# One core: routing one-hots of five groups on GpSimd, copies of the transposed inverse and of the scores on ScalarE

## The chip, the core and the metric

The program runs on one core of one Trainium2 chip. Four engines compute in it: TensorE (PE in the rows; its weight loads are PEld), VectorE (DVE), ScalarE (ACT) and GpSimd (POOL). SyncE (SP) issues most of the transfers. Each engine works through its own list of instructions strictly in order and waits on semaphores for the others. The metric is the device time of one execution in microseconds (us), the median of several runs. Less is better.

## What is computed

Three stages follow one another; the second needs all of the first only through the routing, and the third needs the second.

```python
# 1. delta-rule attention: 4 batches, 8 heads, 768 steps, head width 48
for t in range(S):
    kt, vt, bt = k_n[:, :, t], v[:, :, t], beta[:, :, t, None]
    y[:, :, t] = einsum('bhd,bhde->bhe', q[:, :, t], state)
    v_old = einsum('bhde,bhd->bhe', state, kt)
    state = state + bt[..., None] * einsum('bhd,bhe->bhde', kt, vt - v_old)
# 2. mixture of 8 experts, one expert for a token, tokens with x @ w_skip <= 0 pass through
out[do_compute] = xc + gate * (relu(xc @ w1[e]) @ w2[e])     # e = argmax(xc @ w_gate)
# 3. a wide layer over all 3072 tokens
h = relu(x @ w_in);  return (h * h) @ w_out
```

## The kernel before

**Attention.** The 768 steps are cut into 12 chunks of 64, and two chunks make a group, so there are six groups, 0 to 5. The recurrence inside a chunk is turned into a triangular system. For each group the program needs the inverse of 32 x 32 triangular blocks, all of them at once across the 128 partitions. `inv(g,jj)` builds it row by row on VectorE: 31 steps, each of them a multiplication into `it` (L213) and a subtraction from `T` (L214), and every one waits for the one before it. `T` is first set to the identity by two GpSimd memsets (L195), and its buffer is the one in which `Dg` stood, so the memsets wait for the transposition `At` (L188) that reads `Dg`. After the last step `back` transposes `T` to `X` (L226) and scales it (L227); `back3` transposes it again to `Tn` (L234) and then copies `Tn` in eight pieces into `TX` (L238): four quadrants `qd`, two chunks `j`. `mg` makes the off-diagonal blocks in two rounds of small matmuls: the first (L249) needs `X`, ScalarE copies its result to `M` (L254), and the second (L251) needs `M` and `TX`. `e1` (L260) and `e2` (L272) then make the matrices of each chunk, `sstep` (L288) and `ystep` (L301) carry the state and the output, and `xnat` (L307) brings the output of one batch of the group into token order.

**Two groups ahead** the same loop prepares keys and queries: `norm` (L114 to L124, mostly on GpSimd, from `raw`, a single buffer that a SyncE transfer fills, L88), `scale` (L130), `kp` (L138), `trk`, `trq`, `gp` (L172, with the mask L177 on GpSimd behind the copy L176).

**Routing.** `xnat` ends in `scores` (L435, a sum over the heads on VectorE), a copy of the nine scores of each token into `xn` (L309) and a copy of the token itself (L310); `xn` goes to memory by L311. When all four batches of a group are there, `group` finds the expert of each token: `oh` (L447), then `rk` by matmul (L450 to L454), the rank of each token (L457), and then two rounds, h = 0 and 1, of four one-hot tiles `O` (L466, 128 x 128 in f16, `is_equal` of an iota with the rank). Each `O` is the weight of two small matmuls into `pi` (L468). `O` has one buffer, so the second round waits for the matmuls of the first. `pi` is added to `slots` (L469). The routing of group g stands among the work of group g+1; that of group 5 stands at the end of the attention, and the first gather of the experts waits for it.

**What sets the order.** `PLANS` gives the order in which the pieces of a group are written, `merge` interleaves them with the 31 steps of the next inverse by `WEIGHT`, and then the framework's scheduler sorts the instructions of every engine by a timeline of its own. So whoever moves one instruction to another engine also moves others. `nc.any` leaves the engine to the framework; it divided the 48 copies at L238 into 24 on ScalarE and 24 on VectorE.

**Experts and wide layer.** From about 400 us on, matmuls on TensorE fill the time (L582 to L584, three products for each, for the split of f32 into two parts).

Of the kernel before, what the change touches and what calls it, by code (L numbers as in the profile page):

```python
# [6 lines left out]
B,H,S,D=4,8,768,48  # L7
# [7 lines left out]
WEIGHT={'e': 1.67, 'f': 0.255, 'T': 0.057, 'Q': 0.295, 'G': 6.868, 'S': 1.411, 'Y': 2.496, 'X': 2.685}  # L15
NL=5
NPOOL=1
ENG='gggv v aaav'.split()
KX0='a'; KT0=1; TQ0=0; CA=3; CS=13
EARLY=2  # L20
C=64; NCH=S//C; NG=NCH//2; PR=H//2; BP=B*PR
# [39 lines left out]
def attention(tc, q,k,v,beta, xd, c, scores, group_done):  # L61
    nc=tc.nc
    ident,mU,mb,i48=c['ident'],c['mU'],c['mb'],c['i48']
    with ExitStack() as ctx:
# [7 lines left out]
        TX=P1.tile([128,2,BP,2,64],F32,name="tx")  # L72
# [11 lines left out]
        def e_(x): return {'v':nc.vector,'g':nc.gpsimd,'a':nc.any}[x]  # L84
# [54 lines left out]
        def kxload(g,j,bh):  # L139
            ch=2*g+j  # L140
            for hp in range(2):
                r=slice(64*hp,64*hp+64)
                e_(ENG[0][(2*j+bh)%len(ENG[0])] if g else KX0).tensor_copy(KX[ch%2][r,HB[bh],64*(1-hp):64*(1-hp)+D],ST[ch]['KP',bh][r,:,0:D])
        def trk(g,b):
# [75 lines left out]
        def back(g):  # L220
# [5 lines left out]
            nc.vector.transpose(X.rearrange("p c i -> p i c"),T)  # L226
            e_(ENG[1] if g else 'v').tensor_tensor(T,T,bm.unsqueeze(1).to_broadcast([128,32,32]),op=ALU.mult)  # L227
            st['X']=X
        def back3(g,qd):
            T=G[g]['T']; hp,blk=qd//2,qd%2; r=slice(32*qd,32*qd+32)  # L230
            tn=G[g].setdefault('Tn',None)
            if tn is None:
                tn=P1.tile([128,2*BP,32],F32,tag="sq",name=f"Tn{g}")
                G[g]['last']=nc.vector.transpose(tn.rearrange("p c m -> p m c"),T.rearrange("p i m -> p m i"))  # L234
                G[g]['Tn']=tn
            for j in range(2):
                ST[2*g+j]['TX']=TX[:,j]
                e_(ENG[2][qd] if g else 'a').tensor_copy(TX[r,j,:,hp,32*blk:32*blk+32],tn[r,j*BP:(j+1)*BP])  # L238
        def mg(g,bh):
            st=G[g]; H8=HB[bh]; pp=pE if g==0 and bh else pM  # L240
            for stage in (1,2):
# [61 lines left out]
        def xnat(g,b):  # L303
            xT=G[g]['xT']; last=g==NG-1
            tp=pS.tile([128,PR,128],F32,tag="mm",name=f"tx{g}_{b}")
            for p in range(PR):
                nc.tensor.matmul(tp[:,p,0:105],xT[:,b*PR+p],c['RW'][:,p],start=True,stop=True)  # L307
            xn=P2.tile([128,DX],F32,tag="E2",name=f"xn{g}_{b}")
            nc.vector.tensor_copy(xn[:,DM:],scores(g,b,tp[:,:,96:105]))  # L309
            nc.scalar.copy(xn[:,0:DM].rearrange("p (a d) -> p a d",d=2*D),tp[:,:,0:2*D])  # L310
            c['lastx']=nc.sync.dma_start(xd[0:B*S].rearrange("(b g t) f -> g b t f",b=B,t=128)[g,b],xn)  # L311
            if b==B-1: group_done(g,pS,P2)
# [42 lines left out]
        for qd in range(4): back3(0,qd)  # L355
# [62 lines left out]
class Routing:  # L418
# [14 lines left out]
    def scores(s,g,b,ps):  # L433
        if g not in s.lg: s.lg[g]=s.P.tile([128,B,9],F32,tag="lg",name=f"lg{g}")
        s.nc.vector.tensor_reduce(s.lg[g][:,b],ps.rearrange("p a e -> p e a"),axis=AX.X,op=ALU.add)  # L435
        return s.lg[g][:,b]
    def group(s,g,P,pm,P2):
        nc,rc,V=s.nc,s.rc,s.nc.vector; lg=s.lg[g]; H2=CAP//128; E9=E+1
        def t(n,sh,dt=F32): return P.tile(sh,dt,tag=n,name=f"{n}{g}")
# [6 lines left out]
        r=t('r',[128,B]); V.tensor_reduce(r,val,axis=AX.X,op=ALU.max)  # L446
# [16 lines left out]
        pi=pi[:,0:H2*E].rearrange("p (a b) -> p a b",b=E)  # L463
        for h in range(H2):
            O=P.tile([128,B,128],F16,tag="O",name=f"OH{g}_{h}")
            for b in range(B): V.tensor_scalar(O[:,b],rc['io'][:,128*h:128*h+128],s.rank[:,g,b:b+1],None,op0=ALU.is_equal)  # L466
            for b in range(B):
                for w in range(2): nc.tensor.matmul(pi[:,h],O[:,b],rh[:,b,w],start=b==0 and w==0,stop=b==B-1 and w==1)  # L468
        s.last=V.tensor_tensor(s.slots if g<NG-1 else s.idx,s.slots,pi,op=ALU.add)  # L469
# [453 lines left out]
```

## Time and profile before

| what | value |
|---|---|
| three runs | 989.68, 991.57 (median), 996.97 us |
| the profiled execution | 987.27 us, of which 985.5 us lie between the first and the last instruction (the span) |
| busy: TensorE, VectorE, ScalarE, GpSimd | 880.8, 634.2, 454.1, 278.3 us |
| mean granted TensorE clock | 0.938 of full speed |
| six routings: one-hots at L466 | 48 on VectorE, 240/248/751 ns least/median/most |

The rows further down come from the page and the trace of the profiled execution. Times are in us from the start of the span. "Busy" is the time in which an engine executed something; "x" is a count. In a row of waits, the engine and the line that waited stand left of the arrow, and what ended the wait stands right of it. POOLq, DVEq and SPq are the sequencers that issue for these engines.

### The profile page before, as it was taken

What the parts mean: (1) busy time and instruction counts of PE and PEld (TensorE: products, weight loads), DVE (VectorE), ACT (ScalarE), POOL (GpSimd) and SP (SyncE); (2) the same over time, 40 slices, a digit from 0 to 9 for tenths busy, and PEclk for the clock granted to TensorE, in tenths of its full rate; (3) what the DMA queues carried; (4) which work ended last, traced back from release to release, by engine and by line L of the source; (5) the groups of instructions that cost most, each with busy time, mean ns of one, the idle gap of its engine ahead of it and who ended that gap; (6) DMA issues with size and microseconds to landing.
All of it is one profiled execution on the core that took longest, in us unless ns stands there. A gap on an engine that the chain in (4) does not pass through costs nothing.

```text
span 985.5 us, 20218 instructions
## 1 busy us (share of the span) xinstructions
PE 880.8 (89%) x7820; PEld 814.9 (83%) x7820; DVE 634.2 (64%) x1546; ACT 454.1 (46%) x913; POOL 278.3 (28%) x395
## 2 busy tenths in 40 slices
PE   3369799988989888599999999999999999999994
PEld 3369689878878787589999899899999999998994
DVE  6798999988797922597887999633533433433332
ACT  4455466646654332366566577523332332333221
POOL 7676754353221100576313120220200300200001
PEclk9776988989999959599999999999999999999997
DMA  6773766857664625776857676310100200100000
GB/s 102 95 96 61 141 112 135 144 122 144 125 125 95 138 50 134 260 252 203 277 198 245 208 233 201 101 54 1 53 14 1 65 1 1 41 1 8 25 0 35
DMA packets 182134, 105.83 MB, mean 107 GB/s; under 512 B 154086, under 2 KB 166406, under 8 KB 182034
## 3 DMA queue, kind: packets, MB, share of 16 engines
q1 hardware_dynamic: 150418, 76.73, 32.3%
q0 software_dynamic: 5504, 16.75, 5.3%
q10 hardware_dynamic: 26112, 11.02, 5.3%
q8 instruction: 64, 1.05, 0.5%
q14 instruction: 36, 0.29, 0.1%
HBM read 60.85 MB, written 19.06 MB: 81 GB/s over the span
## 4 chain that ended last, share of the span: by engine, by line
PE 37%; issue 14%; DVE 6%; DMA 4%; ACT 2%; POOL 1%; SPq 0%; POOLq 0%; ACTq 0%; DVEq 0%
PE mh L582 4%; PE mh L584 4%; PE mh L583 4%; PE o L583 4%; PE o L584 4%; PE o L582 4%; PE h L582 2%; PE h L584 2%; PE h L583 2%; PE y L584 2%; PE y L582 2%; PE y L583 2%; DMA raw<-in_moe_w_dram 2%; PE e L260 1%; DVE wl L563 1%
## 5 line engine op out<-in xcount | busy, mean ns | idle before, releaser
L736 DVE TENSOR_TENSOR r<-r 128x512 f32<-128x512 f32 x80 | 55.4, 692 | 169.6 <-ACT gh L735 166.0
L733 ACT ACTIVATE r<-mh 128x512 f32<-128x512 f32 x96 | 57.3, 597 | 212.3 <-PE mh L584 204.9
L583 PE MATMUL o<-wl,gh 128*128 128x384 f32 x384 | 128.8, 338 | 0.0
L582 PE MATMUL o<-wh,gh 128*128 128x384 f32 x384 | 128.4, 337 | 0.0
L582 PE MATMUL mh<-x2h,wh 128*128 128x512 f32 x288 | 115.6, 401 | 0.5 <-ACT r L733 0.5
L583 PE MATMUL mh<-x2l,wh 128*128 128x512 f32 x288 | 113.1, 393 | 0.0
L584 PE MATMUL mh<-x2h,wl 128*128 128x512 f32 x288 | 112.9, 394 | 0.0
L413 POOL DMA_INDIRECT out_dram<-os,rows x24 | 24.4, 1017 | 297.6 <-DVE os L762 236.8
L584 PE MATMUL o<-wh,gl 128*128 128x384 f32 x384 | 89.7, 337 | 0.0
L582 PEld LDWEIGHTS o<-wh,gh 128*128 128x128 f32 x384 | 72.0, 188 | 3.6
L583 PEld LDWEIGHTS o<-wl,gh 128*128 128x128 f32 x384 | 72.0, 188 | 3.5
L584 PEld LDWEIGHTS o<-wh,gl 128*128 128x128 f32 x384 | 69.8, 188 | 3.3 <-DVE gl L737 0.2
L737 DVE TENSOR_TENSOR gl<-r,gh 128x512 fp32r<-128x512 f32 x96 | 66.3, 690 | 5.5
L213 DVE TENSOR_TENSOR it<-At,T 128x31 f32<-128x31 f32 (+15 forms) x155 | 64.3, 415 | 8.3 <-POOL T L195 5.4
L563 DVE TENSOR_TENSOR wl<-raw,wh 128x512 fp32r<-128x512 f32 x96 | 63.1, 700 | 5.9 <-ACT wh L562 4.9
L172 PE MATMUL gp<-KQ,ktx 128*128 128x128 f32 x384 | 57.8, 306 | 8.5 <-ACT ktx L155 6.0
L214 DVE TENSOR_TENSOR T<-T,it 128x31 f32<-128x31 f32 (+15 forms) x155 | 62.9, 406 | 3.3
L260 PE MATMUL e<-KP,tx 128*128 128x112 f32 x384 | 62.0, 315 | 1.5 <-ACT E L262 1.0
L735 ACT ACTIVATE gh<-r 128x512 fp32r<-128x512 f32 x96 | 60.9, 635 | 2.3
L584 PEld LDWEIGHTS mh<-x2h,wl 128*128 128x128 f32 x288 | 53.9, 188 | 9.6
L582 PEld LDWEIGHTS mh<-x2h,wh 128*128 128x128 f32 x288 | 54.2, 188 | 9.1 <-ACT r L733 1.3
L172 PEld LDWEIGHTS gp<-KQ,ktx 128*128 128x128 f32 x384 | 52.4, 216 | 10.6 <-ACT ktx L155 6.6
(253 smaller groups left out, 2081.7 us busy)
## 6 DMA issues: line engine op xcount, KB each, us to landing
raw<-in_moe_w_dram SPq DMA_DIRECT2D x30, 768.0 KB
L<-E ACTq DMA_DIRECT2D x96, 112.0 KB
raw<-in_moe_w_out_dram SPq DMA_DIRECT2D x16, 384.0 KB
L<-E SPq DMA_DIRECT2D x48, 112.0 KB
xd<-xn SPq DMA_DIRECT2D x24, 196.5 KB
raw<-in_k_dram SPq DMA_DIRECT2D x24, 192.0 KB
qn<-in_q_dram SPq DMA_DIRECT2D x12, 384.0 KB
KP<-kn SPq DMA_DIRECT2D x48, 96.0 KB
```

Of the source, the lines that this page charges most:

```text
L172: nc.tensor.matmul(ps[:,p],w,KQ[:,j,p],start=True,stop=True)
L213: e.tensor_tensor(tv,At[:,jj,jj+1:32].unsqueeze(2).to_broadcast([128,n,m]),T[:,jj,0:m].unsqueeze(1).to_broadcast([128,n,m]),op=ALU.mult)
L214: return e.tensor_tensor(T[:,jj+1:32,0:m],T[:,jj+1:32,0:m],tv,op=ALU.subtract)
L260: nc.tensor.matmul(ps[:,p,0:112],st['TX'][:,b*PR+p].rearrange("p h t -> p (h t)"),st['KP',b//2][:,b%2*PR+p],start=True,stop=True)
L563: eng.tensor_tensor(lo[:,sl],r[:,sl],f32v(hi)[:,sl],op=ALU.subtract)
L582: nc.tensor.matmul(out,ah,bh,start=first,stop=False)
L583: nc.tensor.matmul(out,ah,bl,start=False,stop=False)
L584: return nc.tensor.matmul(out,al,bh,start=False,stop=last)
L733: nc.scalar.activation(r,pp,AF.Relu)
L735: nc.scalar.activation(gh,r,AF.Square)
L736: z=nc.vector.tensor_tensor(r,r,r,op=ALU.mult) if n else nc.scalar.activation(r,r,AF.Square)
L737: (nc.gpsimd if n==0 and GLP=='g' else nc.vector).tensor_tensor(gl,r,f32v(gh),op=ALU.subtract)
```

## The change

It does four things. At L466 the one-hots of groups 0 to 4 are made by GpSimd; those of group 5 stay on VectorE. At L238 the copies of quadrants 0, 1 and 2 go to ScalarE by name and those of quadrant 3 to VectorE, for groups 1 to 5 (group 0 is left to the framework as before). At L309 the copy of the scores into `xn` goes from VectorE to ScalarE. A table `ENG` loses the entry that the new lines replace.

```diff
-ENG='gggv v aaav'.split()
+ENG='gggv v'.split()
...
-                e_(ENG[2][qd] if g else 'a').tensor_copy(TX[r,j,:,hp,32*blk:32*blk+32],tn[r,j*BP:(j+1)*BP])
+                o,i=TX[r,j,:,hp,32*blk:32*blk+32],tn[r,j*BP:(j+1)*BP]
+                if g==0: nc.any.tensor_copy(o,i)
+                elif qd<3: nc.scalar.copy(o,i)
+                else: nc.vector.tensor_copy(o,i)
...
-            nc.vector.tensor_copy(xn[:,DM:],scores(g,b,tp[:,:,96:105]))
+            nc.scalar.copy(xn[:,DM:],scores(g,b,tp[:,:,96:105]))
...
-            for b in range(B): V.tensor_scalar(O[:,b],rc['io'][:,128*h:128*h+128],s.rank[:,g,b:b+1],None,op0=ALU.is_equal)
+            for b in range(B): (V if g==NG-1 else nc.gpsimd).tensor_scalar(O[:,b],rc['io'][:,128*h:128*h+128],s.rank[:,g,b:b+1],None,op0=ALU.is_equal)
```

The lines behind L238 stand three lower in the changed kernel (L466 is L469 there). VectorE's list loses 10 of its 24 copies at L238, so that 14 are left there and 34 stand on ScalarE. The lists of all engines differ from the routing of group 0 on. Three places matter below.

GpSimd, where the inverse of group 2 has been used and that of group 3 begins (`KP_1` are masks for the keys of group 4, `T_2631` is the `T` of group 3, `raw_2617` and `sq` belong to the norm of group 5). Before:

```order
L130 TENSOR_TENSOR kn<-raw_1787,ss_2327 128x16x48
L177 TENSOR_TENSOR KP_1_2176<-KP_1_2176,mU 128x4x64
L177 TENSOR_TENSOR KP_1_2179<-KP_1_2179,mU 128x4x64
L195 MEMSET T_2631 128x1024
L195 MEMSET T_2631 128x32
L114 TENSOR_TENSOR sq_0_2743<-raw_2617 128x768
L115 TENSOR_TENSOR sq_0_2743<-sq_0_2743 128x16x24
```

And the same engine and place in the changed kernel:

```order
L114 TENSOR_TENSOR sq_0_2743<-raw_2617 128x768
L115 TENSOR_TENSOR sq_0_2743<-sq_0_2743 128x16x24
L115 TENSOR_TENSOR sq_0_2743<-sq_0_2743 128x16x12
L115 TENSOR_TENSOR sq_0_2743<-sq_0_2743 128x16x6
L115 TENSOR_TENSOR sq_0_2743<-sq_0_2743 128x16x3
L116 TENSOR_TENSOR sq_0_2743<-sq_0_2743 128x16
L117 TENSOR_TENSOR ss_2742<-sq_0_2743 128x16
L114 TENSOR_TENSOR sq_8_2758<-raw_2617 128x768
L177 TENSOR_TENSOR KP_1_2176<-KP_1_2176,mU 128x4x64
L177 TENSOR_TENSOR KP_1_2179<-KP_1_2179,mU 128x4x64
L195 MEMSET T_2631 128x1024
```

The first half of the norm of group 5 and the first operation of its second half now stand ahead of the two masks and of the memsets of `T`; the second memset follows three rows later, behind an L115 and an L121. On SyncE the four transfers into `raw_2617` moved ahead of the loads of `qn` and `z`, behind which they stood.

ScalarE at the same boundary, behind the transposition `Tn` of group 2 (`M_2_0` are the copies between the two rounds of small matmuls). Before:

```order
L292 COPY z_178<-s_1_2135 48x8x48 x2
L254 ACTIVATE M_2_0_2471<-m_2_0_0_2469 32x512
L254 ACTIVATE M_2_0_2471<-m_2_0_1_2470 32x512
L238 COPY tx<-Tn_2459 32x16x32 x4
L176 COPY KP_1_2176<-gp_3_2443 128x4x64
L302 COPY xT_1914<-y_1_2156 128x8x64
```

And now:

```order
L160 COPY KQ_3_2273<-tq_3_2317 128x4x2x64
L162 COPY QT_3_2323<-tq_3_2317 128x4x2x64
L240 COPY tx<-Tn_2459 32x16x32 x6
L257 ACTIVATE M_2_0_2471<-m_2_0_0_2469 32x512
L257 ACTIVATE M_2_0_2471<-m_2_0_1_2470 32x512
L305 COPY xT_1914<-y_1_2156 128x8x64
L312 COPY xn_0_2187<-lg_2188 128x9
```

The copies of `Tn` are six and stand ahead of `M`; before, they were four and stood behind it.

TensorE at the routing of group 2, among the work of group 3 (`pi` with `OH_0`, the first round; `s_1` is the state). Before:

```order
L288 MATMUL s_1_3270<-z_178,L_164 48x48 x7
L468 LDWEIGHTS OH_0_3226
L468 MATMUL pi_3225<-rh_3222,OH_0_3226 128x8
L468 LDWEIGHTS OH_0_3226
L468 MATMUL pi_3225<-rh_3222,OH_0_3226 128x8
L468 LDWEIGHTS OH_0_3226
L468 MATMUL pi_3225<-rh_3222,OH_0_3226 128x8
```

And now:

```order
L291 MATMUL s_1_3270<-z_178,L_166 48x48 x3
L252 MATMUL m_3_1_1_3373<-X_3185,A_1942 32x32
L252 MATMUL m_3_1_1_3373<-X_3185,A_1941 32x32
L252 MATMUL m_3_1_1_3373<-X_3185,A_1942 32x32
L263 MATMUL e_6_0_3447<-KP_0_1935,tx 128x112 x2
L471 LDWEIGHTS OH_0_3226
L471 MATMUL pi_3225<-rh_3222,OH_0_3226 128x8
L471 LDWEIGHTS OH_0_3226
L471 MATMUL pi_3225<-rh_3222,OH_0_3226 128x8
L263 MATMUL e_6_0_3447<-KP_0_1935,tx 128x112 x2
L263 MATMUL e_7_0_3467<-KP_0_1938,tx 128x112 x4
```

The pairs of `pi` matmuls, one pair for each one-hot tile, stood together and are now spread between other matmuls.

## Rows read from the trace of the kernel before

**Rows 1.** Busy by stretch: PE, PEld, DVE, ACT, POOL; then clock, DMA share, GB/s
```profile
80.00:133.00 53.00, 46.67 (x596) 43.37 (x595) 47.49 (x106) 27.66 (x58) 30.61 (x50) 0.83 0.65 117
294.00:345.00 51.00, 44.41 (x814) 40.88 (x812) 42.44 (x127) 22.10 (x45) 6.77 (x10) 1.00 0.51 113
```
**Rows 2.** VectorE busy by stretch, line 213 alone, then line 214 alone
```profile
80.00:133.00 53.00, 14.65 (x31) 0.83 0.65 117
294.00:345.00 51.00, 10.72 (x31) 1.00 0.51 113
...
80.00:133.00 53.00, 15.87 (x31) 0.83 0.65 117
294.00:345.00 51.00, 10.95 (x31) 1.00 0.51 113
```
**Rows 3.** Line 234, ends of the inverses: ns least/median/most, first and last start
```profile
L234 DVE STREAM_TRANSPOSE Tn<-U x1: 2055/2055/2055, 76.3 to 76.3; 128x1024 f32<-128x1024 f32 x1
L234 DVE STREAM_TRANSPOSE Tn<-T x1: 2080/2080/2080, 130.0 to 130.0; 128x1024 f32<-128x1024 f32 x1
...
L234 DVE STREAM_TRANSPOSE Tn<-T x2: 2072/2082/2093, 291.0 to 341.7; 128x1024 f32<-128x1024 f32 x2
```
**Rows 4.** VectorE busy from 80 to 345: line 466, line 238, line 309
```profile
80.00:345.00 265.00, 6.42 (x32) 0.93 0.63 125
...
80.00:345.00 265.00, 8.86 (x20) 0.93 0.63 125
...
80.00:345.00 265.00, 4.81 (x18) 0.93 0.63 125
```
**Rows 5.** Instructions by line: ns least/median/most, first and last start, forms
```profile
L516 POOL TENSOR_SCALAR ol<-io,lo x24: 590/712/1653, 429.4 to 458.6; 128x128 f16<-128x128 f16 x24
...
L238 ACT COPY tx<-Tn x24: 608/614/619, 78.4 to 345.6; 32x512 f32<-32x512 f32 x24
...
L118 ACT ACTIVATE ss<-ss x10: 215/217/229, 40.8 to 210.1; 128x16 f32<-128x16 f32 x10
```
**Rows 6.** TensorE's waits from 130 to 405: us in total, times, longest
```profile
PE pi L468 <- DVE OH L466: 3.3, 3, 2.0
```
**Rows 7.** Order of time: start, us, engine, line, operation; the first inverse steps of two groups
```profile
140.52 1.47 POOL L114 TENSOR_TENSOR sq<-raw 128x768 f32<-128x768 f32 x1
140.61 1.42 DVE L213 TENSOR_TENSOR it<-At,T 128x31 f32<-128x31 f32 x1 [1.20 <-POOL T L195]
...
193.88 0.19 DVE L213 TENSOR_TENSOR it<-At,T 128x31 f32<-128x31 f32 x1 [1.20 <-POOL T L195]
...
203.80 1.00 DVE L213 TENSOR_TENSOR it<-At,T 128x220 f32<-128x220 f32 x1
```
**Rows 8.** Order of time, 184 to 202: ScalarE, TensorE, GpSimd and SyncE at the boundary
```profile
183.97 2.05 PE L172 MATMUL gp<-KQ,ktx 128*128 128x128 f32 x16
184.34 1.20 ACT L254 ACTIVATE M<-m 32x512 f32<-32x512 f32 x2
185.25 1.48 POOL L130 TENSOR_TENSOR kn<-raw,ss 128x768 f32<-128x768 f32 x1 [0.50 <-PE gp L172]
186.37 2.40 ACT L238 COPY tx<-Tn 32x512 f32<-32x512 f32 x4 [0.83 <-DVE Tn L234]
188.10 1.85 PE L251 MATMUL m<-tx,M 32*32 32x32 f32 x56
189.25 1.86 POOL L177 TENSOR_TENSOR KP<-KP,mU 128x256 f32<-128x256 f32 x2 [2.52 <-ACT KP L176]
190.80 4.78 SPq L88 DMA_DIRECT2D raw<-in_k_dram  x4
192.68 1.16 POOL L195 MEMSET T<- 128x1024 f32 x2 [1.57 <-DVE xn L309]
196.60 1.47 POOL L114 TENSOR_TENSOR sq<-raw 128x768 f32<-128x768 f32 x1 [2.76 <-DMA raw<-in_k_dram]
201.68 1.72 POOL L114 TENSOR_TENSOR sq<-raw 128x768 f32<-128x768 f32 x1
```

## The prediction

> **What bounds the kernel now.** The change touches the attention, the first 400 us, so I read the busy time by stretch first, with one inverse in each stretch. In the first stretch shown TensorE is busy for 46.67 of 53 us and VectorE for 47.49, in the last one for 44.41 and 42.44 of 51; ScalarE has 22 to 28 us, GpSimd 30.61 in the first and 6.77 in the last [rows 1]. So two engines are nearly full, and neither is full: each works through its list in order and waits now and then for the other. Behind 400 us TensorE works on the experts and the wide layer. None of the moved work lies there, so what the attention gains or loses moves the end by the same amount.
>
> The second look is at the inverse, the longest chain on VectorE. Its 31 steps are the same work in every group, and yet the two lines of a step are busy for 14.65 + 15.87 = 30.5 us in the first stretch and for 10.72 + 10.95 = 21.7 us in the last [rows 2]. GpSimd is what differs: 30.61 us of work against 6.77 [rows 1]. The order of time shows how: the first step of one inverse, 128 x 31, takes 0.19 us in one group and 1.42 us in another, where it starts 0.09 us behind a GpSimd operation of 1.47 us and ends with it [rows 7]. That gives a price: (30.5 - 21.7) / (30.61 - 6.77) = 0.37 us of VectorE for one us of GpSimd.
>
> The third look is at what such a loss is worth. From one `Tn` to the next the program takes 130.0 - 76.3 = 53.7 us in the first stretch and 341.7 - 291.0 = 50.7 us in the last [rows 3]. An inverse that is 8.8 us lighter came with a period that is 3.0 us shorter, so 0.34 of what VectorE saves arrives. The stretches differ in other work too, so the true share may be anything from 0 to 1; I take 0.34, because both ends come from the same five periods.
>
> **The change, part by part.** (1) VectorE is relieved. Between 80 and 345 us lie the one-hots of groups 0 to 3, 32 of them, with 6.42 us; 20 copies at L238 with 8.86 us, of which 10 go, 4.4 us; and 18 copies of scores with 4.81 us, which all go [rows 4]. Together 15.6 us. The one-hots of group 4 come behind the last inverse, where VectorE has time, so I count them at nothing on VectorE; if there were no such time, 8 x 0.20 = 1.6 us more would be saved.
>
> (2) GpSimd gets the one-hots. The trace of before has no `is_equal` at L466 there, but it has the same shape and type at L516: 0.59 us at least, 0.71 in the middle, 1.65 at most [rows 5]. In the same stretch that is 32 x 0.71 = 22.7 us more of GpSimd. By the price of 0.37, VectorE gives back 8.4 us. The lower bound is 0 (all one-hots fall beside work that they do not disturb), the upper one a full hold each time, 32 x 0.59 = 18.9 us. I take 8.4, the price that this kernel's own inverses paid. VectorE then keeps 15.6 - 8.4 = 7.2 us, and 0.34 of it arrives: **-2.5 us**, with bounds of -15.6 and +3.3.
>
> What the row shows of the hold in full, a step of 0.19 us that takes 1.42, is what the Trainium skill states as a rule: in "SBUF — State Buffer", section "SBUF: two separate sides", the port pair that VectorE and GpSimd share is a lock held for the whole instruction, and a VectorE operation with two SBUF inputs loses against a GpSimd operation that reads SBUF and started first. By that rule alone every one-hot would hold up an inverse step in full, and this term would be +1.1 us; the trace agrees for the one step and shows 0.37 on average.
>
> (3) TensorE waits for the one-hots in another way. Four tiles took VectorE 4 x 0.20 = 0.8 us and take GpSimd 4 x 0.71 = 2.8 us, so each of the two rounds of a group ends 2.0 us later: 4 us in a group, 20 us in five. Behind a late tile stands TensorE's whole list: the `pi` matmuls wait in order, and with them the state, `e1`, `e2` and the keys. The cover is the work between the pairs, and the new order spreads the pairs for that. In the second round of group 2's routing, 32 small matmuls (1.85/56 = 0.033 us each) and 8 large ones (2.05/16 = 0.13 us each) stand between the last pair of the first round and the last three pairs [rows 8]: 2.1 us against 2.8. So 0.7 us of wait is left in a group, 3.5 in five. Before, this wait was 3.3 us [rows 6]. The difference is **+0.2 us**, with bounds of -3.3 (all covered) and +17 (nothing covered).
>
> (4) The identity for the inverse of group 3 comes later. GpSimd now does the norm of group 5 ahead of the memsets of `T`. The norm needs `raw`; its transfers can go when L130 has read the old content, at 185.25 + 1.48 = 186.7, no longer at 190.80 behind the loads of `qn` and `z`. From issue to the norm's first operation passed 196.60 - 190.80 = 5.8 us, so it starts at 192.5. Its first half takes 201.68 - 196.60 = 5.1 us; then follow 1.72 (second half, first operation), 1.86 (two masks) and 1.16 (memsets): `T` is ready at about 202.3 [rows 8]. The first step stood at 193.88, so it comes 8.4 us later. Some of this returns, for the ten steps up to 203.80 ran under that very norm, in 9.9 us; with 21.7/30.5 of that, 7.0 us, they save 2.9 [rows 2, 7]. The inverse ends 5.5 us later, and with the share of 0.34 that is **+1.9 us**; bounds 0 and +8.4. What is late next is `X` of group 3 and with it the small matmuls of that group.
>
> (5) ScalarE gets 10 x 0.614 = 6.1 us of copies and 24 small ones. For these the nearest row is a 128 x 16 activation with 0.217 us, 5.2 us in all [rows 5]. ScalarE idles half of each stretch, and most of the 11.3 us lies there. One place does not hide it: behind `Tn` of group 2 six copies of 0.60 us now precede `M`, so `M` ends at 186.37 + 3.6 + 1.2 = 191.2, where the second round of small matmuls started at 188.10 [rows 8]. That is 3.1 us later with TensorE's list behind it; again at 0.34, **+1.0 us**, bounds 0 and +3.1. The scores' copy of the last group adds 0.2 us at the end of the attention, which I leave out.
>
> **The sum.** -2.5 + 0.2 + 1.9 + 1.0 = +0.6 us on the profiled execution's 987.27, that is 987.9. That execution lies 4.3 us under the median of the three runs and 2.4 under the lowest; I add half of the 4.3 and forecast **990 us**. About 1%, 10 us, is what a measurement here can tell from no change.
>
> **The rivals.** *VectorE sets the pace (0.20).* Then its 15.6 us arrive in full, the one-hots disturb little, and only the late identity is paid: -15.6 + 1.9 = -13.7, about 976 us. For it: 47.49 of 53 us busy. Against it: the period moved by only 3.0 us where the inverse moved by 8.8 [rows 2, 3].
>
> *Every one-hot holds a step (0.12).* VectorE gives back 18.9 us instead of 8.4, the term is +1.1 instead of -2.5, and the time 994 us. For it stands the step of 1.42 us, against it the average price of 0.37. This is the rule of the page named above.
>
> *The late identity counts in full (0.08).* If the inverse of group 3 sets the pace of its period, +8.4 stands for +1.9: about 997 us. Against it: TensorE has 44 to 47 us of work of its own in a stretch [rows 1].
>
> *TensorE waits for GpSimd's one-hots (0.13).* If nothing covers the 4 us in each of five groups, 20 - 3.3 = 17 us are added: 1007 us, slower. It decides once more than 2.6 us in a group are uncovered, which tiles of 1.2 us would do; at L516 they reach 1.65 [rows 5]. Against it: the pairs stand apart now.
>
> *Forecast (0.47).* The parts cancel as in the sum, 982 to 998 us.
>
> **Chances and range.** Faster by over 1%: the first rival, and a little of the forecast's lower edge: 0.22. Slower by over 1%: the last rival, with the edges of the late identity: 0.17. Within 1%: 0.61. The range goes from 975, near the first rival's time, to 1002, short of the last one's; about 0.2 is left out.
>
> **What would show it.** The one-hots on GpSimd between 0.6 and 0.9 us; a larger mean favours the last rival. The wait of `pi` for `OH` near 3.5 us in all. The first inverse step of group 3 some 8 us behind the end of its `At`, and `M` of group 2 behind six copies. VectorE's two inverse lines heavier by 1 to 3 us in a group. The distance from one `Tn` to the next shorter by half a microsecond to one, and longer from group 2 to group 3. I would be wrong if the distances shrank by 3 us each, or if TensorE's idle time grew at L468.

## The result and the profile of the changed kernel

The changed kernel takes **1001.0 us** (median of 4 runs, 994.3 to 1005.7) where the kernel before, on the same chip, took 990.6. The ratio is 1.0112, with a 95% interval of 1.0069 to 1.0155: slower by about 1.1%. The forecast was 990 us and no change that can be told. The range of 975 to 1002 holds the time, but only just and by luck: the sum of +0.6 us is too small, and none of its terms is what made the kernel slower. Runs over 1.5% above the fastest of their kernel count in no ratio and no mean clock below; `after_fixed` loses most by that, 4 of 12, and over all 12 its clock would be 0.937.

The profiled execution took 994.3 us, 7.0 more than the profiled one of before. Its attention ends, with the last addition to the slots, at 407.0 us and not at 402.3. So 4.7 of the 7.0 us lie in the attention, and 2.3 behind it. This is the fastest of the four runs, with a clock of 0.935 where the four have 0.929, so its views show less than the whole loss.

The first view to read is the busy time over the attention, from the first `Tn` to that last addition. The columns are those of [rows 1]. The kernel before:

```profile
76.30:402.30 326.00, 286.38 (x4458) 265.49 (x4453) 250.82 (x703) 165.26 (x332) 104.83 (x160) 0.89 0.59 118
```

And the changed kernel:

```profile
76.30:407.00 330.70, 291.45 (x4438) 268.72 (x4433) 238.78 (x629) 174.08 (x366) 128.21 (x200) 0.88 0.58 116
```

VectorE, the third pair, was relieved of 250.82 - 238.78 = 12.0 us, much as intended. But TensorE's idle time stayed: 326.00 - 286.38 = 39.6 us before and 330.70 - 291.45 = 39.3 after. What grew is TensorE's busy time, by 5.1 us, and its matmuls are the same. The granted clock is what differs, 0.89 and 0.88; busy time times clock is 254.9 and 256.5, the same work within the rounding of the clock. So these two rows say that the relief of VectorE shortened TensorE's waits by nothing in sum, and that TensorE's work took longer at a lower clock.

Where VectorE's time went shows in its own waits between 130 and 405 us. The columns are us in total, times, longest. Before:

```profile
DVE lg L435 <- PE tx L307: 16.2, 7, 6.7
DVE E L275 <- PE e L272: 12.0, 9, 3.7
```

After (the lines behind L238 have numbers higher by three):

```profile
DVE lg L438 <- PE tx L310: 32.4, 14, 9.9
DVE E L278 <- PE e L275: 23.3, 9, 7.8
```

In these two rows VectorE waits 27.5 us longer. Other waits got shorter, and over all rows of the view it waits 62.1 us before and 76.2 after, 14.1 more. The work that it lost became waiting.

The stretches of [rows 1] in the changed kernel, in the same columns:

```profile
80.00:133.00 53.00, 46.02 (x564) 42.49 (x561) 45.79 (x102) 26.90 (x56) 30.71 (x50) 0.81 0.63 113
294.00:345.00 51.00, 44.09 (x722) 39.69 (x722) 38.56 (x108) 23.18 (x49) 12.91 (x20) 0.90 0.42 95
```

In the last one VectorE went from 42.44 to 38.56 us, and the clock from 1.00 to 0.90.

### The profile page after: what moved, and what is told of

Read it like the earlier page. It is cut to its first block, busy times and chain, and to the rows that moved or that the text cites. A ratio compares the mean times of both kernels' runs of the same rounds, so it can differ in the third digit from the quotient of the medians.

```text
span 992.5 us, 20226 instructions
## 1 busy us (share of the span) xinstructions
PE 883.4 (89%) x7820; PEld 815.1 (82%) x7820; DVE 622.5 (63%) x1472; ACT 462.4 (47%) x947; POOL 300.1 (30%) x435
## 4 chain that ended last, share of the span: by engine, by line
PE 48%; DVE 21%; issue 15%; DMA 8%; ACT 5%; POOL 2%; SPq 0%; POOLq 0%; DVEq 0%; ACTq 0%
DVE it L213 4%; PE mh L585 4%; PE mh L587 4%; PE mh L586 4%; PE o L586 4%; PE o L587 4%; PE o L585 4%; DVE T L214 3%; PE e L263 3%; PE e L275 2%; PE tx L310 2%; PE gp L172 2%; DMA raw<-in_moe_w_dram 2%; DMA L<-E 2%; PE y L304 2%
## 5 line engine op out<-in xcount | busy, mean ns | idle before, releaser
L213 DVE TENSOR_TENSOR it<-At,T 128x31 f32<-128x31 f32 (+15 forms) x155 | 64.8, 418 | 6.3 <-POOL T L195 2.8
L214 DVE TENSOR_TENSOR T<-T,it 128x31 f32<-128x31 f32 (+15 forms) x155 | 63.9, 412 | 3.6
L177 POOL TENSOR_TENSOR KP<-KP,mU 128x256 f32<-128x256 f32 x48 | 39.5, 827 | 73.1 <-ACT KP L176 72.6
```

What stands on the lines that cost most here:

```text
L177: nc.gpsimd.tensor_tensor(pv,pv,mU.unsqueeze(1).to_broadcast([128,PR,64]),op=ALU.mult)
L213: e.tensor_tensor(tv,At[:,jj,jj+1:32].unsqueeze(2).to_broadcast([128,n,m]),T[:,jj,0:m].unsqueeze(1).to_broadcast([128,n,m]),op=ALU.mult)
L214: return e.tensor_tensor(T[:,jj+1:32,0:m],T[:,jj+1:32,0:m],tv,op=ALU.subtract)
```

## The experiments

Each ratio is to the kernel before, run beside it on the same chip. The clock is the mean granted TensorE clock over the runs that count; for the kernel before it was 0.939 to 0.942 beside all of them, and it is 0.929 for the changed kernel.

| run | what it is | ratio, 95% interval | clock |
|---|---|---|---|
| oh_only | one-hots on GpSimd alone | 1.0032 [1.0001, 1.0064] | 0.935 |
| tx_only | copies of `Tn` alone | 1.0115 [1.0070, 1.0161] | 0.934 |
| xn_only | copy of the scores alone | 1.0050 [1.0018, 1.0082] | 0.935 |
| no_tx | the change without the copies of `Tn` | 1.0171 [1.0135, 1.0208] | 0.930 |
| after_fixed | the change, old order held | 1.0056 [1.0013, 1.0099] | 0.942 |
| b_afterorder | before, new order held | 1.0151 [1.0084, 1.0217] | 0.930 |
| oh_only_fixed | one-hots alone, old order held | 1.0170 [1.0123, 1.0218] | 0.930 |
| tx_only_fixed | copies of `Tn` alone, old order held | 1.0110 [1.0057, 1.0164] | 0.939 |
| b_fixed | control: before, own order held | 1.0035 [0.9993, 1.0076] | 0.938 |
| a_same | control: the change, own order held | 1.0110 [1.0041, 1.0178] | 0.930 |
| a_txlate | a_same, copies of `Tn` behind `M` | 1.0159 [1.0102, 1.0217] | 0.931 |
| a_mend | a_txlate, first steps ahead as well | 1.0323 [1.0268, 1.0379] | 0.921 |
| b_warm | before, four pauses filled | 1.0068 [1.0036, 1.0100] | 0.943 |
| a_warm | the change, four pauses filled | 1.0028 [0.9998, 1.0059] | 0.949 |
| a_warm2 | the change, three pauses filled | 1.0002 [0.9970, 1.0034] | 0.946 |
| b_warm2 | before, three pauses filled | 1.0018 [0.9986, 1.0050] | 0.943 |
| oh_warm | oh_only, four pauses filled | 1.0040 [1.0001, 1.0080] | 0.937 |
| a_else | the change, filled where there is no pause | 1.0132 [1.0082, 1.0181] | 0.934 |

### The parts one by one

The edits are single lines of the change. Those of oh_only and of xn_only, against the kernel before:

```diff
-            for b in range(B): V.tensor_scalar(O[:,b],rc['io'][:,128*h:128*h+128],s.rank[:,g,b:b+1],None,op0=ALU.is_equal)
+            for b in range(B): (V if g==NG-1 else nc.gpsimd).tensor_scalar(O[:,b],rc['io'][:,128*h:128*h+128],s.rank[:,g,b:b+1],None,op0=ALU.is_equal)
...
-            nc.vector.tensor_copy(xn[:,DM:],scores(g,b,tp[:,:,96:105]))
+            nc.scalar.copy(xn[:,DM:],scores(g,b,tp[:,:,96:105]))
```

tx_only has the four lines of the change at L238 and nothing else; no_tx has the old line there and the rest of the change.

> The kernel before with one part of the change alone: the one-hots of groups 0 to 4 on GpSimd; the copies of the transposed inverse and of the scores stay as before. Theory O (the one-hots on GpSimd carry the loss of 1.1%, by a later `slots` or by GpSimd's list): ratio to before 1.008 to 1.014, and a one-hot's matmul waiting for GpSimd by over 3 us a group. Theory T (the copies of Tn by name on ScalarE, ahead of M, carry it): 0.995 to 1.003 here. Theory L (what costs is the new order of the lists, whichever part brings it): in this kernel the list of VectorE has 27 instructions between the Tn of group 2 and the first inverse step of group 3, where before had 9 and the whole change has 15, and the second memset of T stands behind an L121 of the norm; so the distance of the Tn of groups 2 and 3 grows by 3 us or more, and the ratio is 1.003 to 1.012 though the one-hots themselves wait for nothing.

> The kernel before with one part alone: three of four copies of Tn by name on ScalarE, the fourth on VectorE. Theory O: 0.995 to 1.002. Theory T: 1.007 to 1.013, with the copy M of group 3 at least 3 us later behind its Tn than before. Theory L: VectorE's list has 18 instructions between the Tn of group 2 and the first step of group 3 (before 9), and M stands behind the six copies only at group 3 (group 2 has M first here); 1.002 to 1.008, with the growth at the group whose list got longer and not at the others.

> The kernel before with one part alone: the copy of the nine scores on ScalarE. Theories O and T: 0.995 to 1.002. Theory L: the lists at the ends of the groups read nearly as before (9 or 10 instructions between Tn and the first step, M ahead of the copies of Tn in groups 1 to 4), so 0.993 to 1.001; a gain is possible, since 24 copies of 0.25 us leave VectorE and ScalarE has room. A fourth theory, X (the copy of the scores waits on ScalarE for VectorE's sum and holds what stands behind it), gives 1.004 to 1.010.

> The changed kernel with the copies of Tn left to the framework as before: one-hots on GpSimd and copy of the scores on ScalarE. Theory O: 1.008 to 1.014, as the whole change. Theory T: 0.995 to 1.002. Theory L: here GpSimd's norm stands behind the memsets of T again but for one L115, so the first step of group 3 is not held back by it; 0.998 to 1.006. If the parts simply add, this run is the product of the two parts alone.

No part alone is faster than before. The copies of `Tn` cost 1.15%. The copy of the scores measured 1.0050, although it takes 24 operations from VectorE and the theory of the order expected 1.001 at most. For the one-hots 1.0032 is no more than a control with nothing moved will show further down (b_fixed, 1.0035), so a loss by them alone isn't shown. And the parts don't add: one-hots and scores alone give 1.0032 x 1.0050 = 1.0082, together (no_tx) 1.0171, and with the copies of `Tn` added, which alone cost 1.15%, the whole is back at 1.0112. No part carries the loss as a price that adds up. In no_tx one place stands out, the keys and masks of group 3 (the `KP_1` in the lists of the change belong to group 3, not to group 4 as it says there), in order of time:

```profile
198.36 1.75 PE L172 MATMUL gp<-KQ,ktx 128*128 128x128 f32 x14
203.69 0.22 ACT L118 ACTIVATE ss<-ss 128x16 f32<-128x16 f32 x1 [3.10 <-POOL ss L117]
203.81 0.35 ACT L176 COPY KP<-gp 128x256 f32<-128x256 f32 x1
207.51 1.92 DVE L188 STREAM_TRANSPOSE At<-Dg 128x1024 f32<-128x1024 f32 x1
```

`At` starts at 207.51, where it started at 190.62 before. Most of that comes from TensorE's list: the last products `gp`, from which `At` is made, stand behind two of the `tx` and start at 198.36, where they started at 183.97 [rows 8]. The norm adds to it: its square root (L118) waits 3.10 us for GpSimd, and the copy `KP` behind it on ScalarE comes only at 203.81. Both come from the new order; from the lists of TensorE and ScalarE nothing was moved away. Here the pauses themselves got longer. From the first `Tn` to the last addition, in the columns of the first view, TensorE is idle for 49.9 us, against 39.6 before, at an unchanged 0.89:

```profile
76.60:415.10 338.50, 288.65 (x4458) 265.34 (x4452) 244.05 (x638) 169.34 (x357) 126.92 (x200) 0.89 0.57 113
```

### The two orders held

For these runs a table of the old (or new) order binds each instruction that the change does not move to its neighbours on the same engine. The binding sets the order of issue and waits for nothing.

```diff
         full(tc, *args)
+        keep_order(tc)
...
+def keep_order(tc):
+    ins=list(tc.nc.cur_bb.bb.instructions)
...
+            if prev is not None: tc.add_manual_dep(i,prev.name,mybir.DependencyInfo(mybir.DependencyClass.NoSync,mybir.DependencyReason.DATA),reason="order")
```

> The changed kernel, all three parts of the change in it, but every instruction that was not moved to another engine is bound to the place that it had in the kernel before (a table of the old order, as pure issue-order edges between neighbours of one engine, no waits). Only the moved one-hots and copies are placed freely. Theory L (the loss is that of the new order, and the moved work itself is worth what VectorE is relieved of): 0.992 to 1.000, the distances of the Tn at or under those of before, the granted clock no lower. Theories O, T and X (the moved work itself costs): 1.007 to 1.014, as the whole change. In between, 1.002 to 1.006, both would hold a part.

> The reverse: the kernel before, with every engine as it was, but each instruction that the change does not move bound to the place that it has in the changed kernel. Theory L: 1.008 to 1.018, since VectorE has the old load and the new order, with the At of group 3 near 196 us and not 190.6. Theories O, T and X: 0.997 to 1.004.

> One part alone with the old order held: the one-hots of groups 0 to 4 on GpSimd. Theory L: 0.994 to 1.000, under the 1.003 of the same part with the order free; the matmuls that need a one-hot wait for GpSimd for a few us in all. Theory O: 1.003 or more.

> One part alone with the old order held: six copies of Tn a group by name on ScalarE, placed freely; the other instructions stand as before, so that M comes ahead of the copies in groups 1 to 4 as it did. Theory L: 0.996 to 1.002, against 1.0115 with the order free. Theory T in the form that the longer row of copies on ScalarE itself delays what follows: 1.004 or more, with the second round of small matmuls at least 1 us later behind Tn than before.

The four corners are old work in the old order 1, new work in the old order 1.0056, old work in the new order 1.0151, and both new 1.0112. So the new order with every engine as it was costs as much as the whole change or more, and there the clock is 0.930. The new work in the old order has a clock of 0.942 in the runs that count, and yet gains nothing. The theory that the moved work is worth a gain once the order is held falls with that. The attention of after_fixed shows why, in the columns of the first view:

```profile
76.60:406.80 330.20, 291.24 (x4458) 269.06 (x4452) 238.08 (x629) 173.41 (x366) 128.35 (x200) 0.89 0.58 116
```

VectorE is relieved of 12.7 us in the old order too, and TensorE is idle for 39.0 us, against 39.6 before. Its busy time is longer by 4.9 us, at a clock that the rounding to 0.89 can't tell from that of before.

Why one-hots on GpSimd need another order shows in oh_only_fixed, in order of time:

```profile
162.16 2.49 POOL L466 TENSOR_SCALAR OH<-io,rank 128x128 f16<-128x128 f16 x4
164.71 0.21 PE L468 MATMUL pi<-rh,OH 128*128 128x8 f16 x2 [0.37 <-POOL OH L466]
164.95 0.17 DVE L469 TENSOR_TENSOR slots<-slots,pi 128x16 f32<-128x16 f32 x1 [1.93 <-PE pi L468]
```

Four tiles take GpSimd 2.49 us; in the old order the addition to the slots stands early in VectorE's list and waits for them, and inverse steps wait behind it (the next one started at 165.04). From 130 to 405 us VectorE waits 12.1 us at this line in oh_only_fixed and 5.0 in oh_only, where the scheduler put the addition later:

```profile
DVE slots L469 <- PE pi L468: 12.1, 4, 8.9
...
DVE slots L469 <- PE pi L468: 5.0, 2, 4.7
```

So for this part the order that the scheduler made for it goes with 1.0032, and the old order with 1.0170. The wait at the slots is longer by 7.1 us; that the difference comes from it is argued, not shown. The copies of `Tn` cost the same in both orders (1.0110 and 1.0115). In tx_only the second round of small matmuls starts 9.8, 6.6, 9.6 and 8.3 us behind `Tn` in groups 2 to 5, where it started 3.9, 4.3, 6.4 and 7.5 us behind it before. In tx_only_fixed, where `M` stands ahead of the copies in groups 1 to 3 as before, it starts at most 0.8 us later than before in groups 1 to 4. So a late second round is not what costs the 1%, and neither is the longer row of copies by delaying it, which theory T priced at 1 us or more. What does cost it in tx_only_fixed, at a clock of 0.939, stays open.

### Mending the new order

The two controls hold a kernel's own order, so that nothing moves. a_txlate then changes only the table of ScalarE's order, where `M` goes ahead of the copies of `Tn`; a_mend changes the tables of VectorE and GpSimd as well, where the first steps of the inverse and the memsets go ahead of other work.

> A control: the kernel before with the table of its own order, so the same instructions in the same order with the same waits. Every theory: 0.997 to 1.003. It gives a second profile of this program: if the granted clock is a property of the program, TensorE has its full clock from 245 to 345 us again (0 us at the lower level); if it is chance, some 5 to 40 us at the lower level, as in the profiles of the other kernels.

> The other control: the changed kernel with the table of its own order, nothing else. Every theory: 1.007 to 1.014, as measured for the changed kernel. Its profile shows whether the pause of TensorE ahead of the first round of small matmuls of group 4 (2.2 us at 290 us) and ahead of the `tx` of group 2 (2.95 us at 247 us) come again, and the lower clock behind them.

> The changed kernel in its own order, but for one thing: on ScalarE the six copies of Tn of the groups 2 to 5 stand behind the two copies M of their group (and behind the xT and KP copies in between), not ahead of them. Theory T (these copies hold M and xT, TensorE pauses for them and its clock falls): 1.002 to 1.007, the pause ahead of the `tx` of group 2 (2.95 us) under 1 us. Theory L in the form that VectorE's order (sums of the scores and the identity of T ahead of the first steps) makes the loss: 1.008 to 1.013, as the control.

> As the run before, and in addition on VectorE the first four steps of the inverses of groups 3 and 4 stand ahead of the sums and of the start of the routing that the changed kernel puts first, and on GpSimd the two masks and the two memsets of T of group 3 stand ahead of the norm, as in the kernel before. If late M and the late first steps are the two causes: 0.996 to 1.003, the first step of group 3 under 12 us behind its Tn (16.4 in the changed kernel, 9.7 before). If the loss lies elsewhere: 1.006 or more.

The two controls hold: 1.0035 [0.9993, 1.0076] for the same instructions in the same order, which is also the size of difference below which nothing is read here, and 1.0110 for the changed kernel again. In a_txlate the edit did what it says, in order of time:

```profile
186.32 2.10 DVE L234 STREAM_TRANSPOSE Tn<-T 128x1024 f32<-128x1024 f32 x1
188.66 1.20 ACT L257 ACTIVATE M<-m 32x512 f32<-32x512 f32 x2
189.88 3.44 ACT L240 COPY tx<-Tn 32x512 f32<-32x512 f32 x6
191.80 1.19 PEld L254 LDWEIGHTS m<-tx,M 32*32 32x32 f32 x34
```

`M` starts 2.3 us behind `Tn`, and the second round of small matmuls 5.5 us behind it (in the changed kernel 5.8 and 7.9). It brought nothing: 1.0159. In a_mend the first step of group 3's inverse comes 3.2 us sooner behind `Tn` than in a_same (13.2 us for 16.4; under 12 was expected), and the kernel loses 2% more than a_same:

```profile
203.40 0.22 ACT L118 ACTIVATE ss<-ss 128x16 f32<-128x16 f32 x1 [7.14 <-POOL ss L117]
203.64 0.59 ACT L305 COPY xT<-y 128x512 f32<-128x512 f32 x1
204.28 2.03 PE L310 MATMUL tx<-RW,xT 128*128 128x105 f32 x8 [5.10 <-ACT xT L305]
```

I had put the norm behind the memsets on GpSimd, but ScalarE's list still had the norm's root ahead of `xT`. ScalarE waits 7.14 us, and TensorE pauses 5.10 us for `xT`. So a_mend doesn't tell what late first steps cost by themselves; it shows that a list changed alone can make TensorE pause where the other lists don't fit it. The same root of the norm held ScalarE in no_tx.

### Is it the clock?

The kernel before gives a price without any edit. Of the 108 of its runs that count the quarter with the lowest clock (mean 0.935) took 990.0 us, the quarter with the highest (0.947) 982.8. A clock lower by 0.012 goes with 7.2 us, and 0.012 is about what the changed kernel lost (0.929 for 0.941). To see whether the clock is a cause, I filled pauses of TensorE with matmuls that nobody reads, into a PSUM tile that the next matmul overwrites, with the order of all else held:

```diff
+def fill(nc,c,dst,n):
+    for _ in range(n): FILLS.append(nc.tensor.matmul(dst,c['ident'],c['ident'],start=True,stop=True).ins)
...
+FILLS=[]; WARM={'tx': {(2, 2): 10}, 'rk': {0: 8}, 'm': {4: 6}, 'etp': 0}
...
+            fill(nc,c,tp[:,0],WARM['tx'].get((g,b),0))
             for p in range(PR):
                 nc.tensor.matmul(tp[:,p,0:105],xT[:,b*PR+p],c['RW'][:,p],start=True,stop=True)
```

This is a_warm2; the numbers of `WARM` say at which group and batch how many stand, and `etp` is the place ahead of the experts, 20 in a_warm and 0 here. In a_else it reads:

```diff
-FILLS=[]; WARM={'tx': {(2, 2): 10}, 'rk': {0: 8}, 'm': {4: 6}, 'etp': 0}
+FILLS=[]; WARM={'tx': {(2, 1): 8, (3, 1): 8, (5, 1): 8}, 'rk': {}, 'm': {}, 'etp': 0}
```

> The kernel before in its own order, with 42 additional matmuls (identity by identity, 128 columns, into a PSUM tile that the next matmul overwrites; nobody reads them) at four places at which TensorE pauses: 6 ahead of the third `tx` of group 0 (pause 1.4 us), 6 ahead of `rk` of group 1 (1.5 us), 10 ahead of the fourth `tx` of group 4 (2.6 us) and 20 ahead of the first transposition of the experts, where it waits 5.6 us for the gather. They add no work to the answer. Theory C (the lower clock behind the pauses costs the time): fewer us at the lower clock between 130 and 410 us, the fall at 347 us (23.9 us long) gone or shorter, ratio 0.975 to 0.995. Rival S (the clock only goes along with the pauses, and the pauses are what costs): 0.999 to 1.006, the added matmuls costing up to their own 5 us where TensorE does not pause.

> The changed kernel in its own order, with 44 such matmuls at the places where it pauses: 8 ahead of `rk` of group 0, 10 ahead of the third `tx` of group 2, 6 ahead of the first round of small matmuls of group 4, 20 ahead of the first transposition of the experts. Theory C: ratio to the kernel before 0.985 to 1.005, at least 0.6% under the changed kernel's 1.011, with the falls of the clock at 150, 248 and 294 us gone. Rival S: 1.009 to 1.017.

> The changed kernel in its own order, with the 24 matmuls that nobody reads at three places of the attention (8 ahead of `rk` of group 0, 10 ahead of the third `tx` of group 2, 6 ahead of the first round of small matmuls of group 4) and none ahead of the experts. Theory C: 0.996 to 1.003. Rival S: 1.006 to 1.014, the gain of the run before having been made elsewhere.

> The kernel before in its own order, with 20 such matmuls: 6 ahead of the third `tx` and 6 ahead of `rk` of group 0, 8 ahead of `rk` of group 1, where its two profiles show pauses of 1.4 to 3.9 us; none elsewhere. Theory C: 0.990 to 1.000, the falls of the clock at 142 and 207 us gone. Rival S: 1.000 to 1.006.

> The kernel with the one-hots on GpSimd alone, in its own order, with 27 such matmuls: 6 ahead of the third `tx` and 6 ahead of `rk` of group 0, 8 ahead of the first round of small matmuls of group 2, 7 ahead of the third `tx` of group 2, where its profile shows pauses of 1.35 to 2.3 us. Theory C: 0.990 to 1.000, under the 1.003 without them. Rival S: 1.003 to 1.010.

> The changed kernel in its own order, with 24 of the matmuls that nobody reads at three places at which its profile shows TensorE at work without a pause: 8 each ahead of the second `tx` of groups 2, 3 and 5, which follow their neighbours within 0.1 us. Theory C (it was the filled pauses): 1.010 to 1.020, the 24 matmuls costing their own 3 to 6 us or nothing, and the lower clock staying as it was. Rival (any shift of that size would do): 0.997 to 1.006.

The changed kernel goes from 1.0110 in its own order to 1.0028 [0.9998, 1.0059], and to 1.0002 [0.9970, 1.0034] without the filling ahead of the experts. Its clock rises from 0.930 to 0.949 and 0.946. The same number of matmuls at places without a pause leaves it at 1.0132. One place in a_same, with what TensorE did before, and the stretch around it:

```profile
246.79 2.55 PE L310 MATMUL tx<-RW,xT 128*128 128x105 f32 x16 [2.80 <-ACT xT L305]
...
235.00:270.00 35.00, 31.85 (x501) 29.86 (x502) 22.86 (x63) 21.66 (x45) 9.68 (x15) 0.76 0.41 85
```

And the same place in a_warm2 (L63 are the filling matmuls, L316 the same `tx`):

```profile
243.49 2.50 PE L63 MATMUL tx<-ident 128*128 128x128 f32 x20
246.46 2.03 PE L316 MATMUL tx<-RW,xT 128*128 128x105 f32 x16 [0.47 <-ACT xT L310]
...
235.00:270.00 35.00, 33.79 (x598) 31.68 (x599) 29.78 (x78) 24.03 (x51) 13.02 (x20) 1.00 0.64 124
```

TensorE pauses for 2.80 us before `tx` in the first kernel, and in the 35 us around it the granted clock is 0.76. With 2.50 us of useless matmuls in that pause it is 1.00, the higher of the two levels (2.4 GHz; 0.76 is a mean of both), and the next `tx` matmuls take 2.03 us for 2.55. Over the attention:

```profile
76.30:410.00 333.70, 294.75 (x4460) 271.61 (x4455) 236.35 (x630) 173.83 (x366) 128.93 (x200) 0.87 0.57 115
...
76.30:400.10 323.80, 287.07 (x4506) 265.08 (x4501) 235.15 (x628) 173.70 (x366) 127.96 (x200) 0.92 0.60 118
...
76.20:413.20 337.00, 296.21 (x4504) 273.26 (x4498) 239.23 (x628) 174.33 (x366) 128.50 (x200) 0.88 0.57 114
```

These are a_same, a_warm2 and a_else. TensorE does more matmuls in a_warm2 than in a_same and is busy for 7.7 us less, at 0.92 instead of 0.87; the idle time shrinks by 2.2 us only. This is the one cause that the runs show for the loss of the changed kernel: TensorE's clock is lower because of pauses at certain places, and with these filled the loss is gone. It is not the cause of every loss in the table: in no_tx the pauses themselves were longer by 10.2 us. Nor is it shown that the new order costs nothing else: at 0.946 the filled kernel has a higher clock than the kernel before beside it (0.940), and it only reaches the same time.

In the other two kernels filling brought nothing: b_warm and b_warm2 had a clock of 0.943, hardly above the 0.940 to 0.942 of the kernel before, and oh_warm 0.937. So these runs don't test what a higher clock would give them. In b_warm the 20 matmuls ahead of the experts lasted too long: VectorE read the gather's data at 411.16, and TensorE came to them at 412.15, where in the kernel before it was the first to use them. In a_warm TensorE was the first again, 0.1 us ahead of VectorE. No version beats the kernel before.

**What stays open.** Why just these pauses of the new order meet the clock so badly, and those of the old order less, isn't settled; the sum of the pauses is the same. The 2.3 us behind the attention are no mark of the change: in a_same, the changed kernel in its own order, that stretch is longer by 0.9 us only (995.9 us in all and 410.0 at the last addition). Whether after_fixed is slower at all isn't shown, since its 1.0056 [1.0013, 1.0099] overlaps the 1.0035 [0.9993, 1.0076] of the control with nothing moved; that its clock is unchanged isn't shown either.

## Why the prediction was wrong, step by step

**What bounds the kernel.** This is where it failed. I read 46.67 and 47.49 busy us of 53 as two nearly full engines that wait for each other [rows 1], and took from two periods a share of 0.34 by which VectorE's savings arrive [rows 2, 3]. The two stretches differed in TensorE's clock as well, 0.83 and 1.00, in the same rows. The shorter period needed no lighter inverse to explain it. Measured, 12.0 us off VectorE moved TensorE's idle time from 39.6 to 39.3 us, and 12.7 us off it in the old order (after_fixed) moved it to 39.0: a share of nearly zero. The term of -2.5 us, and the shares of 0.34 in (4) and (5), fall with that, and so does the rival "VectorE sets the pace".

**(1) and (2), relief and give-back.** VectorE lost 13.5 us between 80 and 345 us, against 15.6 - 8.4 = 7.2 in the sum. The give-back was mis-sized. The busy time of all engines in that stretch, before and after, in the columns of the first view:

```profile
80.00:345.00 265.00, 236.49 (x3754) 219.19 (x3752) 232.22 (x627) 144.82 (x295) 101.50 (x153) 0.93 0.63 125
...
80.00:345.00 265.00, 236.08 (x3585) 218.39 (x3583) 218.74 (x561) 147.92 (x312) 120.22 (x185) 0.90 0.62 120
```

VectorE's busy time at L213 and at L214 alone, before:

```profile
80.00:345.00 265.00, 64.34 (x155) 0.00 (x0) 0.93 0.63 125
...
80.00:345.00 265.00, 62.88 (x155) 0.00 (x0) 0.93 0.63 125
```

After:

```profile
80.00:345.00 265.00, 64.79 (x155) 0.00 (x0) 0.90 0.62 120
...
80.00:345.00 265.00, 63.91 (x155) 0.00 (x0) 0.90 0.62 120
```

The inverse is heavier by 1.5 us in all, and GpSimd works 18.7 us more there. That is 0.08 us for one us of GpSimd, not 0.37. The price came from the norm, and the one-hots behave otherwise. First all 40 of the changed kernel, then four of them in order of time with an inverse step that ran beside them:

```profile
L469 POOL TENSOR_SCALAR OH<-io,rank x40: 592/600/947, 156.8 to 370.1; 128x128 f16<-128x128 f16 x40
...
257.07 2.70 POOL L469 TENSOR_SCALAR OH<-io,rank 128x128 f16<-128x128 f16 x4 [4.29 <-DVE rank L460]
258.63 0.37 DVE L213 TENSOR_TENSOR it<-At,T 128x156 f32<-128x156 f32 x1
```

Their median of 0.600 us is near the least of [rows 5], not its middle: they are hardly held up themselves. The step took 0.37 us beside them, and one of the same size 0.35 at 206.39, with no one-hot running. The rule of the Trainium skill in "SBUF — State Buffer", section "SBUF: two separate sides", by which each would hold a VectorE step with two SBUF inputs for its whole length, is not borne out for these operations here. What the forecast got wrong by this term was in the kernel's favour, and it was worth nothing. So the rival "Every one-hot holds a step" falls too.

**(3) TensorE waits for the one-hots.** Small, and smaller than said. The 3.3 us of [rows 6] hold 1.4 us for group 5, whose one-hots stay on VectorE; 1.9 us belong to the groups that the change touches. In the changed kernel 1.5 us are left:

```profile
PE pi L471 <- DVE OH L469: 1.5, 2, 1.1
```

These are group 5's again, and no `pi` waits for a one-hot of GpSimd, where 3.5 us were forecast. The rival at 1007 us falls. The time came out near it for another reason.

**(4) and (5), the late identity and `M`.** Both came late, `M` as read off the order and the identity for other reasons. At the place of [rows 8], in order of time:

```profile
186.38 2.08 DVE L234 STREAM_TRANSPOSE Tn<-T 128x1024 f32<-128x1024 f32 x1
188.02 1.47 POOL L114 TENSOR_TENSOR sq<-raw 128x768 f32<-128x768 f32 x1 [0.35 <-DMA raw<-in_k_dram]
188.71 3.42 ACT L240 COPY tx<-Tn 32x512 f32<-32x512 f32 x6
192.16 1.20 ACT L257 ACTIVATE M<-m 32x512 f32<-32x512 f32 x2
192.41 1.97 PE L172 MATMUL gp<-KQ,ktx 128*128 128x128 f32 x16
194.31 2.11 PE L254 MATMUL m<-tx,M 32*32 32x32 f32 x64
196.31 1.99 DVE L188 STREAM_TRANSPOSE At<-Dg 128x1024 f32<-128x1024 f32 x1
198.36 0.95 POOL L195 MEMSET T<- 128x1024 f32 x1 [1.57 <-DVE ss L119]
200.38 0.17 POOL L195 MEMSET T<- 128x32 f32 x1
202.37 0.20 DVE L438 TENSOR_REDUCE lg<-tx 128x9 f32<-128x36 f32 x1 [1.12 <-PE tx L310]
202.77 0.19 DVE L213 TENSOR_TENSOR it<-At,T 128x31 f32<-128x31 f32 x1
```

`M` stands behind six copies, and the second round starts 7.9 us behind `Tn` instead of 3.9. The first step comes at 202.77, 8.9 us later than before (2.2 of them lie ahead of `Tn`), where 8.4 were forecast, but that is luck. The norm was earlier than forecast (188.02, not 192.5), and the memsets had ended at 200.55. `At` itself came 5.7 us later, a move that the forecast didn't have: the last products `gp` stand later in TensorE's list, at 192.41 for 183.97. The step came another 4.5 us behind the end of `At`, held by the sums `lg`. But the distance from this `Tn` to the next is 57.0 us, against 57.4 before: so the +1.9 and +1.0 us do not show in this period. The starts of the second to the last `Tn`, where [rows 3] stood before:

```profile
L234 DVE STREAM_TRANSPOSE Tn<-T x5: 2042/2084/2141, 131.3 to 345.0; 128x1024 f32<-128x1024 f32 x5
```

The first is at 76.3 in both kernels, and the last at 345.0 instead of 341.7: the distances sum to 3.3 us more, not less.

**The term that was missing.** The sum puts TensorE's clock at nothing and gives no reason, although the views that I read show it in every row. With such a term, the question to ask of the new order would have been where TensorE pauses, and not what VectorE saves. Measured, the clock fell from 0.941 to 0.929, which goes with 7.2 us over the runs of the kernel before, and filling three pauses took the whole 1.1% back. The size could not have been read from the one profile of before.

**The chances.** Slower by over 1% had 0.17, from a mechanism that didn't occur. A rival "the new order costs by itself" was missing, although the lists ahead of the prediction show a new order on several engines.

## What to carry to other kernels

Before pricing what an engine saves, take the busy time of the busiest engine times its granted clock over the stretch, and see whether its idle time can shrink at all; a share fitted to two stretches with different clocks says nothing. Where a scheduler sorts all lists anew, test the order apart from the work, by holding the old order with the new work and the new order with the old work. Where TensorE is nearly full, look at its pauses one by one, since a pause of 2.8 us, as the one shown, can be followed by a stretch at a lower clock.

## What the runs showed of the hardware

Useless matmuls in the pauses of a nearly full TensorE made a kernel faster by 1.1% (1.0110 to 1.0002), mostly through the granted clock (0.930 to 0.946; 7.7 us less busy time in the attention and 2.2 us less idle). They did nothing where they stood elsewhere (1.0132), or in two other kernels whose clock they hardly raised. The Trainium skill has the two levels and the return to the lower one when idle in "TensorE: Matmul & The Clock Gate", Part 1 (the clock gate), and calls what the ramp costs under 1% of a typical span. A fall behind a pause shows here too (2.80 us in a_same, then 0.76 over the 35 us around it). And over 108 runs of one kernel, a difference of 0.012 in the mean clock goes with 7.2 us of about 987, so 0.7%, and the attention has a mean clock of 0.87 to 0.92 in the profiles shown.

GpSimd made a 128 x 128 one-hot in f16 in 0.600 us (0.592 at the least) and ScalarE copied 128 x 9 values in 0.20 us; VectorE's inverse lost 0.08 us for a microsecond of GpSimd work added by them, where an operation of the norm with two SBUF inputs had held a single step until 1.42 us had passed [rows 7].
